# A first weight quarter loaded in fp32 and rounded on the chip, a reordered first group, a compact running state and loads tied to progress, in a linear-attention and Mish feed-forward kernel

## The chip, the core and the metric

The kernel runs on one core of a Trainium2 chip. The metric is the device time of one execution in microseconds (us); the time before is 209.66 us, the median of three runs (209.61 to 210.24).

The names used below are those of the profile: PE is TensorE (matmuls; PEld its weight loads), DVE is VectorE, ACT is ScalarE, POOL is GpSimd, SP is SyncE. ACT, SP and POOL also issue DMAs, each in its own queue; only the loads issued by POOL change the type on the way (fp32 in memory, fp16 on the chip).

## The reference

Per batch b (4) and head h (8), with 768 positions of 64 values, lightning attention in blocks with a decay lam[h]:

```
intra = (q_block @ k_block.T) * Dmask            # Dmask[i,j] = lam^(i-j) for i >= j, else 0
out   = intra @ v_block + (q_block * lam^(i+1)) @ state
state = lam^block * state + (k_block * lam^(block-1-i)).T @ v_block
```

The heads are then laid side by side (x: 3072 tokens x 512) and go through

```
h = x @ w_in          # 512 -> 2048
g = h * tanh(softplus(h))          # Mish
out = g @ w_out       # 2048 -> 512, fp32
```

## The kernel before

**Groups.** The sequence is cut into six groups n = 0..5 of 128 positions (C); a group has one chunk for each of the four batches, chunk number i = 4n + b, so a group is 512 tokens (GT). For each group the loop at line 719 runs 16 units of the first product (`mm1_unit`, ni = 0..15: four matmuls of 512 columns, then ACT's Mish into `hsg`) and then the second product: 16 `mm2_unit` in group 0, and in the later groups 14 `fast_unit`, a scheme with seven instead of eight products whose sums of tokens (`gsum`, line 572) and of weights (`tsum`, line 553) are made by DVE. Everything is in an order written out by hand (`manual_schedule`): each engine executes its instructions in the order in which the program names them. While group n's units run, the attention of group n+1 is made in pieces, put behind the units that the table `room` names; unit u of the loop is an mm1 unit for u < 16.

**First group (lines 682 to 713).** Chunk 0's k and q come in fp32 by SP's and ACT's queues and are rounded by ACT (k0) and DVE (q0). For each chunk c there are three steps: `first_t(c)` transposes k and q on PE, with copies by ACT (pkT) and DVE (pqT); `first_s(c)` makes the scores and DVE multiplies them by the decay mask dm (two sb); `first_o(c)` multiplies by v, and ACT copies the result to x^T (xt). `busy(m)` is m matmuls of 512 columns on zeros. After the steps, the first three chunks' part of units 0 and 1 (`mm1_part`) is done before the loop begins. The tables dm, lk (decay of k), lbc and lbm (decay of the state over a group) are made in between.

**Weights and loads.** w_in's first quarter comes in three parts (win0, line 93), then three more quarters of w_in (line 96) and four of w_out (line 103), all by POOL's queue behind the loads of chunks 0 to 3; then chunks 4 to 7. Group 2's loads (`ahead`) are issued one behind each `att_a` and the rest (v) after group 0's units; those of group n+2 (`later`) behind the units in `times`.

**Running state.** For each batch and half of the heads, `wst[b][hf]` holds two copies of 128 x 256: two pairs of heads, each a block-diagonal 128 x 128, whose blocks off the diagonal are zero. The new state is (pv + old) * lbm: DVE adds (line 302 in group 1, line 393 later: `raw`, 128 x 256), POOL multiplies by lbm (line 304, held back in the list `behind`; line 395 later). In the groups from 2 on, attention goes by pairs of batches: `pair_a` (pv and the state; for n > 2 also `turn` of the chunk two further), `pair_s` (scores; state times q), `pair_o` (times v, scaling to xtok, and a transposing DMA by SP into xt). `turn(i)` is `scale_k(i)`, k times lk, by DVE or POOL according to i (line 264), and two transposing DMAs by SP of q and k.

**PSUM.** The tags ph and po have two buffers each. Unit 2 of every group takes its buffer from po (line 491); the pv of `pair_a` come from po as well while u < 15.

## Time and profile before

| what | us |
|---|---|
| time, median of three runs | 209.66 |
| the profiled execution's own time | 210.5 |
| its span in the profile | 208.5 |
| group 0's first steps, up to the last v product (line 249) | 0 to 19.6 |
| group 0's mm1 units | to 33.9 |
| group 0's mm2 units, with group 1's attention | to about 56 |
| group 1's mm1 units, with group 2's attention | to 75.85 |
| group 1's fast units | to 88.5 |
| groups 2 and 3, each mm1 and fast units | 88.5 to 119.3 and 119.3 to 150.1 |
| groups 4 and 5 | to 208.5 |

Times inside the profile are microseconds from the start of the span. A row of the timeline gives start, duration, engine, line, operation, names and shapes, how many, and in brackets how long the engine stood idle before it and what ended that. A row of the stretches gives, for each engine in the order PE, PEld, DVE, ACT, POOL, the time it was busy and the instructions (x), then the granted TensorE clock as a share of full speed, the mean busy share of the DMA engines and GB/s. A row of the chain gives start, duration and what the chain stood on.

### The profile page before, as it was taken

How to read it: one execution, taken by the hardware profiler on the slowest of the kernel's cores; microseconds unless marked ns; L12 is line 12 of the kernel's file. 1: busy time of each engine (PE TensorE's matmuls, PEld its weight loads, DVE VectorE, ACT ScalarE, POOL GpSimd, SP SyncE). 2: the span in 40 equal slices, each digit the busy share in tenths (PEclk: the TensorE clock that was granted, in tenths of full speed). 3: DMA queues.
4: the chain of work that ended last, by engine and by line, in shares of the span. 5: the costliest groups of instructions: out<-in, count | busy, mean ns of one | idle time of the engine just before them, and what ended most of it. 6: DMA issues, size and time to landing. Idle time of an engine off the chain costs nothing.

```text
span 208.5 us, 4364 instructions
## 1 busy us (share of the span) xinstructions
PE 197.3 (95%) x1736; PEld 128.6 (62%) x1736; DVE 136.5 (65%) x253; ACT 90.2 (43%) x159; POOL 108.5 (52%) x132
## 2 busy tenths in 40 slices
PE   7598999999998999999999999999999999999993
PEld 2366544467644568845578845578755598544892
DVE  5747761577899998546997537995728784222543
ACT  4444768566672532044542055442065520366300
POOL 7997333799999799539997049970000000000000
PEclk9759999999999999999999999999999999999999
DMA  9999999999999399997999994999462222400023
GB/s 128 137 153 176 208 206 195 153 211 131 160 183 165 25 95 137 196 204 157 100 129 148 210 174 69 98 141 199 104 176 53 50 41 75 139 0 3 2 78 124
DMA packets 112470, 26.76 MB, mean 128 GB/s; under 512 B 102594, under 2 KB 111938, under 8 KB 112450
## 3 DMA queue, kind: packets, MB, share of 16 engines
q0 software_dynamic: 78080, 13.37, 87.7%
q1 hardware_dynamic: 31392, 10.49, 26.4%
q10 hardware_dynamic: 2978, 2.62, 4.1%
q8 instruction: 13, 0.21, 0.4%
q14 instruction: 7, 0.06, 0.1%
HBM read 27.26 MB, written 6.29 MB: 161 GB/s over the span
## 4 chain that ended last, share of the span: by engine, by line
PE 73%; DVE 12%; DMA 6%; issue 4%; POOL 2%; ACT 1%; ACTq 0%; DVEq 0%
PE ph L494 28%; PE z L599 13%; PE x L599 8%; PE y L599 7%; PE po L516 6%; DMA vz<-in_v_dram 4%; DVE sb L427 3%; DVE raw L393 2%; DVE xtok L446 2%; DMA qn<-in_q_dram 2%; PE fin L599 2%; DVE gsum L572 1%; PE pO L249 1%; PE pO L438 1%; PE pS L411 1%
## 5 line engine op out<-in xcount | busy, mean ns | idle before, releaser
L494 PE MATMUL ph<-xt,win 128*128 128x512 f16 (+2 forms) x404 | 88.6, 369 | 0.4 <-ACT hsg L508 0.2
L508 ACT ACTIVATE hsg<-ph 128x512 f16<-128x512 f32 x96 | 57.0, 597 | 70.4 <-PE ph L494 70.3
L494 PEld LDWEIGHTS <-win 128*128 128x128 f16 x404 | 37.0, 98 | 37.6 <-issue 0.6
L599 PEld LDWEIGHTS <-gsum 128*128 128x128 f16 x336 | 31.6, 98 | 3.5
L395 POOL TENSOR_TENSOR w<-raw,lbm 128x256 f16<-128x256 f32 x24 | 18.6, 805 | 16.7 <-DVE raw L393 16.7
L427 DVE TENSOR_TENSOR sb<-pS,maskT 128x512 f16<-128x512 f32 x32 | 19.8, 680 | 9.8 <-PE pS L411 9.8
L572 DVE TENSOR_TENSOR gsum<-hsg 128x1024 f16<-128x1024 f16 x20 | 18.6, 932 | 10.9 <-ACT hsg L508 10.9
L599 PEld LDWEIGHTS <-hsg 128*128 128x128 f16 x240 | 23.2, 98 | 3.7
L80 POOL DMA_DIRECT2D vz<-in_v_dram x24 | 21.9, 916 | 4.5 <-DMA win<-in_moe_w_in_dram 2.5
L69 POOL DMA_DIRECT2D kn<-in_k_dram x23 | 21.0, 914 | 4.9 <-DMA win<-in_moe_w_in_dram 2.4
L77 POOL DMA_DIRECT2D qn<-in_q_dram x23 | 20.9, 908 | 4.5 <-DMA wout<-in_moe_w_out_dram 3.3
L599 PE MATMUL x<-wout,hsg 128*128 128x256 f16 x160 | 19.6, 273 | 0.0
L599 PE MATMUL z<-tsum,gsum 128*128 128x256 f16 x160 | 19.1, 272 | 0.0
L264 DVE TENSOR_TENSOR ktil<-kn,lk 128x512 f16<-128x512 f16 (+1 forms) x12 | 11.3, 960 | 6.5 <-DMA kn<-in_k_dram 6.5
L516 PE MATMUL po<-wout,hsg 128*128 128x512 f16 x64 | 15.1, 379 | 0.0
L264 POOL TENSOR_TENSOR ktil<-kn,lk 128x512 f16<-128x512 f16 x12 | 13.2, 1103 | 0.0
L446 DVE TENSOR_TENSOR xtok<-pO,lqt 128x256 f16<-128x256 f32 x32 | 11.3, 412 | 0.9 <-PE pO L438 0.9
L393 DVE TENSOR_TENSOR raw<-pv,w 128x256 f32<-128x256 f32 x24 | 8.6, 414 | 4.6 <-PE pv L385 4.4
L516 PEld LDWEIGHTS <-hsg 128*128 128x128 f16 x64 | 6.0, 98 | 5.9
L599 PE MATMUL z<-tsum,hsg 128*128 128x256 f16 x80 | 9.6, 273 | 0.0
L650 DVE TENSOR_TENSOR u<-z,p 128x512 f32<-128x512 f32 x5 | 3.5, 692 | 9.0 <-PE z L599 9.0
L165 PE MATMUL busy<-kzero 128*128 128x512 f16 x18 | 7.9, 534 | 1.2 <-DVE kzero L150 1.2
(101 smaller groups left out, 220.1 us busy)
## 6 DMA issues: line engine op xcount, KB each, us to landing
out_dram<-osum SPq DMA_DIRECT2D x14, 256.0 KB, 2.5
vz<-in_v_dram POOLq DMA_DIRECT2D x24, 128.0 KB, 5.5
kn<-in_k_dram POOLq DMA_DIRECT2D x23, 128.0 KB, 5.4
qn<-in_q_dram POOLq DMA_DIRECT2D x23, 128.0 KB, 5.5
wout<-in_moe_w_out_dram POOLq DMA_DIRECT2D x4, 512.0 KB, 17.2
win<-in_moe_w_in_dram POOLq DMA_DIRECT2D x3, 512.0 KB, 10.9
out_dram<-osum ACTq DMA_DIRECT2D x5, 256.0 KB, 4.5
out_dram<-osb ACTq DMA_DIRECT2D x4, 256.0 KB, 5.9
```

The source lines that it names most:

```text
L69: nc.gpsimd.dma_start(out=kn[i], in_=chunk_rows(k, i))
L77: nc.gpsimd.dma_start(out=qn[i], in_=chunk_rows(q, i))
L80: nc.gpsimd.dma_start(out=vz[i % NVB][:, :, 0:D], in_=chunk_rows(v, i))
L264: (nc.vector if i <= B or 2 * B < i < 3 * B or i >= (NG - 1) * B else nc.gpsimd).tensor_tensor(out=t, in0=kn[i], in1=bc(lk, 2, D), op=ALU. ...
L395: nc.gpsimd.tensor_tensor(out=wst[b][hf][(n + 1) % 2], in0=raw, in1=lbm[:, hs, :], op=ALU.mult)
L427: nc.vector.tensor_tensor(out=s.sb[m][t], in0=sc[m][t], in1=bc(maskT, 1, JP), op=ALU.mult)
L446: nc.vector.tensor_tensor(out=xtok[m][:, :, t, :], in0=s.pO[t][:, m], in1=bc(lt[:, :, t], 2, D), op=ALU.mult)
L494: nc.tensor.matmul(ph_t[ni][:, lo:hi], win0[min(ni, 2)][:, kc, max(ni - 2, 0) * 128 : max(ni - 2, 0) * 128 + 128] if ni < w else win[ni // ...
L508: nc.scalar.activation(hsg[n][:, ni, :], ph_t.pop(ni), AF.Mish)
L516: nc.tensor.matmul(po, hsg[n][:, ki, b * C : (b + 1) * C], wout[part][:, kk, :], start=(ki == 0), stop=(ki == NKI - 1),)
L572: nc.vector.tensor_tensor(out=gsum[n, i][:, ks, :], in0=a, in1=b, op=op)
L599: nc.tensor.matmul(t, lhs(kk, b), rhs(kk, c, c + w), start=(fresh and kk == 0 and (alone or i == 0)), stop=(kk == HK - 1), skip_group_chec ...
```

## The change

1. **w_in's first quarter.** The three DMAs of POOL are gone. SP issues four DMAs of 128 x 512 fp32 (256 KB each, one for each kc) into `stage` right behind k of chunk 0. DVE rounds kc = 0 and 1 and ACT kc = 2 and 3 into `win[0]`, in the midst of the first steps. The tile `stage` takes one of the two buffers of hsg.
2. **First group.** lk and a new table lbh (lam^128 for every head) are made by ACT before k0; lbc is copied from lbh by DVE, and `pair_decays` goes behind the steps. Seven of the eight decays of the mask stand ahead of q0's rounding, one behind it. The load of the Mish table goes from behind chunk 1's pkT ahead of it. `busy` of 128 columns is added around chunk 0's transposes; of the seven `busy` groups of 512 columns (12 matmuls) two (3 matmuls) stay. Instead, units 0 and 1 are done by chunks of 128 tokens as soon as each chunk's xt is there, and unit 2's first three chunks go behind the last v product.
3. **Compact state.** In groups from 1 on only the blocks on the diagonal are added (`sum_rows`: two DVE instructions of 64 partitions, one for each head of a pair), into a tile `raw` for two batches, and one DVE instruction of 128 x 512 (`next_state`) multiplies it by lbc and writes `state`. POOL's multiplications and `behind` are gone.
4. **scale_k** goes to POOL for i = 5..8 only; i = 12..19, with POOL before, go to DVE.
5. **Loads.** ek's iota goes ahead of q of chunk 1. In groups 1 to 3 each load in `later` has `pace()` ahead of it: POOL copies one element of the latest marked result (an hsg, p1, p7 or u3), and so waits for it. Order within a group: k and q of three chunks first, v later.
6. **Unit 2's buffer** is from po only in groups 0 and 1, else from ph. In group 1 the pieces stand behind the units 6, 8, 11, 12, 16, 20 instead of 6, 8, 9, 12, 13, 17.

The diff, cut to its core:

```diff
-    win0 = [const.tile([128, NKC, b_ - a_], F16, name=f"win0{a_}") for a_, b_ in zip(cuts, cuts[1:])]
+    win = [const.tile([128, NKC, DF // WS], F16, name=f"win{s}") for s in range(WS)]
...
     load_q(0)
+    stage = work.tile([128, 2 * NKC, DF // WS], F32, name="stage", tag="hsg", bufs=2)
+    for kc in range(NKC):
+        nc.sync.dma_start(out=stage[:, kc, :], in_=moe_w_in[kc * 128 : (kc + 1) * 128, 0 : DF // WS])
...
-    for s in range(WS):
+    for s in range(1, WS):
         load_win(s)
...
-        (nc.vector if i <= B or 2 * B < i < 3 * B or i >= (NG - 1) * B else nc.gpsimd).tensor_tensor(
+        (nc.gpsimd if B < i <= 2 * B else nc.vector).tensor_tensor(
...
+    def sum_rows(n, b, pv, j0, nj, olds):
+        if (n, b // 2) not in raws:
+            raws[n, b // 2] = work.tile([128, 2, JP, D], F32, name="raw", tag="raw", bufs=2)
+        raw = raws[n, b // 2]
+        for hp in range(2):
+            rs = slice(64 * hp, 64 * hp + 64)
+            nc.vector.tensor_tensor(out=raw[rs, b % 2, j0 : j0 + nj, :], in0=pv[rs, :, rs],
+                                    in1=olds(rs), op=ALU.add)
+    def next_state(n, p):
+        nc.vector.tensor_tensor(
+            out=state[p][(n + 1) % 2], in0=raws[n, p],
+            in1=lbc.unsqueeze(1).unsqueeze(3).broadcast_to([128, 2, JP, D]), op=ALU.mult)
...
+    def pace():
+        nc.gpsimd.tensor_copy(paced, mark[-1])
...
-            ph_t[ni] = ps.tile([128, GT], F32, name="ph", tag="po" if ni == 2 else "ph", bufs=2)
+            ph_t[ni] = ps.tile([128, GT], F32, name="ph", tag="po" if ni == 2 and n < 2 else "ph", bufs=2)
...
     nc.scalar.activation(k0, kn[0], AF.Copy)
-    decays(0)
+    decays(0, range(JP))
+    decays(1, range(JP - 1))
     nc.vector.tensor_copy(q0, qn[0])
+    decays(1, range(JP - 1, JP))
...
-    first_t(0)
+    busy(2, C)
+    first_t(0, between=4)
     nc.scalar.activation(dm[:, 1], dm[:, 1], AF.Exp)
+    nc.scalar.preload_act_table(AF.Mish)
     busy(1)
+    nc.vector.tensor_copy(win[0][:, 0, :], stage[:, 0, :])
     first_s(0)
-    pair_decays()
-    nc.scalar.activation(lk, lnb, AF.Exp, scale=ek)
-    busy(2)
     first_t(1)
-    nc.scalar.preload_act_table(AF.Mish)
-    busy(1)
+    busy(2)
+    nc.vector.tensor_copy(win[0][:, 1, :], stage[:, 1, :])
+    for kc in (2, 3):
+        nc.scalar.activation(win[0][:, kc, :], stage[:, kc, :], AF.Copy)
     first_s(1)
     first_o(0)
-    busy(3)
     first_t(2)
-    busy(1)
+    for ni in range(2):
+        mm1_part(0, ni, 0, C)
     first_s(2)
     first_o(1)
-    busy(3)
     first_t(3)
+    for ni in range(2):
+        mm1_part(0, ni, C, 2 * C)
+    first_s(3)
     first_o(2)
-    busy(1)
-    first_s(3)
-    mm1_part(0, 0, 0, GT - C)
+    for ni in range(2):
+        mm1_part(0, ni, 2 * C, 3 * C)
     first_o(3)
-    mm1_part(0, 1, 0, GT - C)
+    mm1_part(0, 2, 0, GT - C)
     scale_k(0)
+    pair_decays()
...
-            room = dict.fromkeys((6, 8, 9, 12, 13, 17) if n == 1 else (2, 5, 7, 9, 12, 16), 1)
+            room = dict.fromkeys((6, 8, 11, 12, 16, 20) if n == 1 else (2, 5, 7, 9, 12, 16), 1)
...
             if later and u in times:
+                pace()
                 later.pop(0)()
...
+            if n == 1 and u < 2:
+                next_state(n, u)
             if n == 1 and u < 3:
                 turn((n + 1) * B + 1 + u)
-            while n == 1 and behind:
-                behind.pop(0)()
```

88 lines of the change are left out of this document (40 added, 48 removed).

## Prediction

> **What bounds the kernel now.** I read the page first (busy shares, the chain of work by engine), then the chain in order of time, then the stretches.
>
> ```profile
> PE 197.3 (95%) x1736; PEld 128.6 (62%) x1736; DVE 136.5 (65%) x253; ACT 90.2 (43%) x159; POOL 108.5 (52%) x132
> PE 73%; DVE 12%; DMA 6%; issue 4%; POOL 2%; ACT 1%; ACTq 0%; DVEq 0%
> ```
>
> PE is the bound over the whole, but a busy PE is not a PE at its peak, and 27% of the chain lies elsewhere. So the question is where PE waits. In the chain in order of time:
>
> ```profile
> 1.31 4.05 DMA qn<-in_q_dram
> 5.81 1.05 DVE dm L184 x4
> 9.10 0.18 DVE lnp L192
> 9.41 0.29 ACT lk L694
> 11.81 1.28 PE busy L165 x3
> 15.57 0.65 PE busy L165 x3
> 19.04 0.55 PE pO L249 x7
> 28.68 5.18 PE ph L494 x24
> ```
>
> The first 19.59 us (19.04 + 0.55) are a chain of small steps: a load, decays, small tables, dummy matmuls. From there on PE streams: 24 matmuls of 512 columns in 5.18 us, 0.216 us each, so 0.054 us for 128 columns. The stretches show where it streams less well:
>
> ```profile
> 4.60:8.00 3.40, 1.76 (x19) 1.03 (x20) 2.08 (x7) 1.92 (x4) 3.40 (x5) 1.00 2.32 148
> 8.00:14.85 6.85, 6.02 (x46) 3.86 (x44) 3.39 (x8) 3.36 (x6) 6.85 (x10) 0.50 2.06 142
> 19.60:33.86 14.26, 14.22 (x85) 7.20 (x84) 9.10 (x24) 9.44 (x16) 5.03 (x6) 1.00 1.24 207
> 57.00:75.85 18.85, 16.86 (x164) 8.96 (x163) 18.85 (x29) 9.12 (x16) 17.45 (x21) 1.00 1.18 116
> 88.50:106.40 17.90, 17.30 (x162) 9.05 (x161) 13.05 (x23) 8.87 (x15) 14.26 (x18) 1.00 1.31 152
> 119.30:137.20 17.90, 17.31 (x162) 9.00 (x160) 13.16 (x24) 8.96 (x15) 14.36 (x18) 1.00 1.21 122
> 150.10:166.00 15.90, 15.90 (x145) 7.95 (x143) 9.71 (x18) 8.96 (x15) 0.00 (x0) 1.00 0.44 101
> ```
>
> The last three are the same part (16 units with attention beside) of groups 2, 3 and 4. Group 4 needs no pv, which is 16 matmuls of 128 columns, 0.9 us. So 17.90 - 15.90 - 0.9 = 1.1 us of waiting in each of groups 2 and 3, where the busy column admits 0.60: a tail of each matmul covers part of a gap. In group 1 (57.00 to 75.85) PE is idle 18.85 - 16.86 = 1.99 us by the row; in the same ratio (1.1 to 0.60) that is 3.6 us, and DVE is busy all the time. What PE waits for there:
>
> ```profile
> 62.78 0.38 PE L385 MATMUL pv<-vz,ktil 128*128 128x128 f16 x4 [0.42 <-DMA vz<-in_v_dram]
> 66.02 0.40 PE L411 MATMUL pS<-qraw,kraw 64*128 64x128 f16 x7 [0.40 <-DVE raw L393]
> 91.99 0.38 PE L385 MATMUL pv<-vz,ktil 128*128 128x128 f16 x4 [0.46 <-ACT hsg L508]
> 103.61 0.29 PEld L419 LDWEIGHTS <-qraw 64*128 64x128 f16 x15 [0.24 <-DVE xtok L446]
> 99.27 2.96 DVE L572 TENSOR_TENSOR gsum<-hsg 128x1024 f16<-128x1024 f16 x1
> 99.55 3.26 POOL L395 TENSOR_TENSOR w<-raw,lbm 128x256 f16<-128x256 f32 x4
> ```
>
> The fourth row waits for a scaling that stands behind the fifth: a sum of tokens that takes 2.96 us while POOL's state products (sixth) run. After 150.1 there is almost nothing to win.
>
> **The change, part by part.**
>
> *The first group (term A).* Its root is q of chunk 0. Removed from the chain: lnp and lk with their waits (9.02 to 9.70 in the chain), three of the four decays behind q0 (0.79 us), and most dummy matmuls. But the new limit is what the steps read: the loads of chunks 1 to 3.
>
> ```profile
> 8.14 0.89 POOL L77 DMA_DIRECT2D qn<-in_q_dram  x1
> 9.01 1.78 POOL L80 DMA_DIRECT2D vz<-in_v_dram  x2
> DMA to landing us min/median/max: 4.0/4.8/17.5
> 10.74 2.28 POOL L93 DMA_DIRECT2D win<-in_moe_w_in_dram  x3
> win<-in_moe_w_in_dram POOLq DMA_DIRECT2D x1, 256.0 KB, 6.4
> kn<-in_k_dram POOLq DMA_DIRECT2D x23, 128.0 KB, 5.4
> 15.04 1.29 DVE L239 TENSOR_TENSOR sb<-pS,dm 128x512 f16<-128x512 f32 x2 [0.64 <-PE pS L235]
> ```
>
> The third row is that of q's loads in the first 40 us. So q of chunk 3 is there at 8.14 + 4.0 = 12.1 us, while PE first asks for it behind the dummies that end at 16.2 (15.57 + 0.65): a cover of 4 us, which goes. The four stage DMAs now run ahead of these loads on the same engines. Their price has no row. In the stretch 19.60 to 33.86 w_in and w_out flow at 207 GB/s of fp16, 0.52 MB in 2.5 us, for 1 MB read. In fp32 the read is the same and the write double: 2.5 us if the read limits, 5.0 if the write does, nothing if gaps take it in; I take 2.5, as that row is the same matrix in pieces of the same 2 KB. Then q of chunk 3 comes at 14.6. Behind it: its four transposes (0.22) and their way to DVE (0.17: the row 19.04 has 0.55 for seven matmuls), the copy (0.43), scores (as much as transposes, 0.39), two sb (1.29), units 0 and 1's third part, eight matmuls of 128 columns that now stand ahead on PE (0.4), and the v product (0.55): 18.1 us against 19.59, so 1.5 us. Besides, 24 matmuls of 128 columns of units 0 and 1 are then done (1.3 us) where before four of 384 (0.65) were: 0.7 us. Unit 2's part hides ACT's last xt as unit 1's did. A = 2.2 us. The rounding costs DVE and ACT two instructions each:
>
> ```profile
> 5.38 0.43 DVE L686 CAST q<-qn 128x512 f16<-128x512 f32 x1 [0.82 <-DMA qn<-in_q_dram]
> 4.18 0.63 ACT L684 ACTIVATE k<-kn 128x512 f16<-128x512 f32 x1 [0.79 <-DMA kn<-in_k_dram]
> 5.20 1.09 POOL L77 DMA_DIRECT2D qn<-in_q_dram  x1
> ```
>
> 0.86 on DVE and 1.26 on ACT lie in the wait for chunk 1 and 2's loads, if the stage has landed; behind them on DVE wait the sb, on ACT pkT and xt. That cover is gone if the loads are early; then they are on the chain, with at most 0.86. Bounds of A: 4 us if stage costs the loads nothing and the clock stays full, -0.3 if it costs 5.0.
>
> The third row is POOL's issue during the cast of q0: 1.09 us, where others take 0.89. The Trainium skill, page SBUF — State Buffer, section "SBUF: two separate sides", says that a VectorE copy from fp32 in SBUF can lock GpSimd out of writing descriptors. By it the two casts would put 0.4 us on the loads, and A would be 1.8; the sum does without.
>
> *Later weights.* Three DMAs less in POOL's queue: v of chunk 3, the last ahead of them, lands at about 13.9 (issued 9.9, half of the row 9.01 on, plus 4.0), win0's last part, issued at 12.2, at 18.6: 4.7 us of transfer go and 2.5 come, so all from w_in's second quarter on is 2.2 us earlier, like PE. The tightest is k of chunk 4:
>
> ```profile
> 38.51 0.69 DVE L264 TENSOR_TENSOR ktil<-kn,lk 128x512 f16<-128x512 f16 x1 [6.50 <-DMA kn<-in_k_dram]
> 41.25 0.31 PEld L324 LDWEIGHTS <-ktil 128*128 128x128 f16 x2
> ```
>
> It is ready at 39.20 for a use at 41.25: 2 us of cover. Without the 2.2, A would be lost here by 0.2 only.
>
> *Group 1 and the state (term B).* The costs, POOL's first:
>
> ```profile
> L395 POOL TENSOR_TENSOR w<-raw,lbm 128x256 f16<-128x256 f32 x24 | 18.6, 805 | 16.7 <-DVE raw L393 16.7
> L393 DVE TENSOR_TENSOR raw<-pv,w 128x256 f32<-128x256 f32 x24 | 8.6, 414 | 4.6 <-PE pv L385 4.4
> L572 DVE TENSOR_TENSOR gsum<-hsg x20: 675/682/2960, 69.3 to 193.3; 128x1024 f16<-128x1024 f16 x20
> L264 DVE TENSOR_TENSOR ktil<-kn,lk x12: 681/685/2184, 18.9 to 151.4; 128x512 f16<-128x512 f16 x11, 128x512 f16<-128x512 f32 x1
> ```
>
> For each group POOL loses eight products (6.4 us). DVE has as many sums as before (four of 256 columns for two batches) and two next_state of 128 x 512, which I price as the median ktil, 0.69: 1.4 us. In group 1's own halves two sums of 128 columns (0.26 each, as L184 in the chain) stand for one of 256 (0.41): 0.1 in each of eight halves, 0.9 in all, nothing unless DVE is what comes last there. What comes back: DVE's instructions beside POOL's products take up to three to four times their median (maxima 2960 and 2184). In 57.00 to 75.85 three ktil, four sums of weights and two of tokens are stretched, by some 4 us, against 1.4 added. Of PE's 3.6 us, about 1 is order on PE itself (as in group 4, where short gaps remain), 0.6 is the load of v; of the other 2, which wait for DVE or for a buffer that DVE holds (the new places 11, 16, 20 ease that too), I take B = 1.5; bounds 0 and 3. v's load is 2.2 us earlier as PE is, and POOL issues it without products between.
>
> *Groups 2 and 3 (term C).* Unit 2 in ph frees both po buffers for pv: the wait for hsg (0.46 idle) goes. The sum of tokens in 0.68 instead of 2.96 lets xtok be ready before PE asks, also with next_state ahead of it. DVE gets 2 x 0.69 (next_state) and 2 x 0.69 (scale_k) in 17.90 us, 2.8, and loses 2.3: 13.6 of 17.90 busy, so hidden. Of 1.1 us each I take 0.8: C = 1.6; bounds -1 (DVE's additions reach PE) and 2.2.
>
> *Pacing and scale_k.* A copy of one element and a wait on POOL; behind it wait only loads. POOL's products are gone, so loads are issued at PE's pace. The tightest is k of chunk 15: issued behind u3 of group 1 (row below), at 84.3 to 85.2, landing after the 5.4 of kn's row at about 90, scaled behind the first two sums of group 3's pair_a, at about 92.5 (the pv row 91.99).
>
> ```profile
> 83.58 0.69 DVE L650 TENSOR_TENSOR u<-z,p 128x512 f32<-128x512 f32 x1 [1.12 <-PE z L599]
> ```
>
>  The pacing costs nothing; without that cover, as much as k is late. The marks end with step 3, so the last four loads of a group aren't paced.
>
> *Sum.* A + B + C = 2.2 + 1.5 + 1.6 = 5.3 us. The profiled execution's own 210.5 (span 208.5, 2.0 around it) becomes 205.2; the median is 0.84 below it, so 209.66 - 5.3 = **204.4 us**.
>
> **The rivals.**
>
> 1. *The loads hold the first group* (0.15): stage's transfer costs 5.0 us. A = -0.3, so 206.9. For it: the fp32 write is double. Against: in the row of 207 GB/s the read is already twice that.
> 2. *The clock stays full* (0.14): the row 8.00 to 14.85 has a granted clock of 0.50, after a stretch in which PE was busy 1.76 of 3.40 us. Full clock there, with loads hardly delayed, gives A = 4: 202.6. For it: more matmuls stand in 4.6 to 8. Against: fewer stand after 9. The Trainium skill, page TensorE: Matmul & The Clock Gate, section "Part 1: The HAM clock gate", says that a window of about 3.4 us of sustained work frees the clock and an idle one halves it; the rows agree with such windows (3.40 and 6.85), and by it this rival hangs on the one window from 4.6 us.
> 3. *DVE becomes the bound in the middle* (0.11): stretching is due to POOL's issues too and stays. C = 0, B = 0.5: 207.0. For it: DVE is at 18.85 of 18.85 in group 1. Against: the median of gsum is 0.68 while POOL issues loads most of the time.
> 4. *Slower: a scale_k on DVE waits for a paced load* (0.07). Place: k of chunks 14, 15, 18, 19 in pair_a. Behind it on DVE stand the sums that free PE's pv buffers. It decides from a landing 8 us after the issue; each us beyond is lost in groups 2 and 3. With 4 us: A + B = 3.7 won, C lost, 8 lost: 214.0. For it: landings up to 17.5 us in the qn row. Against: that was behind the weights; the median of kn is 5.4.
>
> **How the numbers follow.** Forecast 0.53, rivals 0.15, 0.14, 0.11, 0.07. The forecast's own range is 202.8 to 206.0. For 8 in 10 I go to rivals 1, 2 and 3, with their bounds: 201.2 to 207.7. All but rival 4 are faster by more than 0.3% (about what a measurement here can tell from no change); with some of 1 and 3 that fall short: faster 0.89, same 0.04, slower 0.07.
>
> **What would show it.** A: the last v product ends near 18 us, q of chunk 3 lands near 14.6, and PE's first wait in the steps is for DMA. B: stretch of group 1's units 2 us shorter, no ktil or gsum over 1 us. C: 16.8 us where 17.90 stand, no wait of pv for hsg. Wrong if: v product after 19.6; DVE waiting for kn; the 17.90 unchanged.

## The result and the profile after

The changed kernel is slower: 211.96 us (median of 9 runs, 210.69 to 213.18) against 210.24 for the kernel before (9 runs, 208.26 to 211.84), a ratio of 1.0122 with a 95% interval of 1.0086 to 1.0158. (The ratio, here and below, compares the executions in the fast state alone, so it is not the quotient of the two medians.) The forecast was 204.4 from 209.66, with a range to 207.7. The profiled execution of the changed kernel took 213.18 us, the longest of its nine; its span is 210.8.

First the page of the changed kernel (busy time and share by engine), which stands against the first row that the prediction shows:

```profile
PE 197.4 (94%) x1753; PEld 129.9 (62%) x1753; DVE 139.0 (66%) x281; ACT 91.2 (43%) x161; POOL 81.7 (39%) x125
```

POOL lost its products as meant (108.5 to 81.7 us), DVE gained 2.5 us, PE does the same work. So the sum of work tells nothing here; only the stretches do. I cut both traces at the same events: the last matmul of the last v product, the last of group 0's mm1 units, and the first mm1 matmul of each later group. The stretches of the changed kernel (length, busy time of PE, PEld, DVE, ACT, POOL, clock, DMA share, GB/s):

```profile
0.00:20.85 20.85, 15.23 (x136) 10.02 (x137) 13.23 (x34) 10.03 (x17) 15.79 (x26) 1.00 1.54 181
20.85:34.61 13.76, 13.60 (x87) 7.03 (x85) 9.45 (x27) 9.19 (x16) 5.26 (x6) 1.00 1.27 205
34.61:55.83 21.22, 20.82 (x179) 12.70 (x178) 13.98 (x33) 13.17 (x29) 19.11 (x21) 1.00 2.18 161
55.83:88.75 32.92, 31.58 (x320) 21.79 (x317) 28.88 (x55) 13.38 (x25) 13.16 (x24) 1.00 1.25 121
88.75:122.36 33.61, 31.49 (x288) 21.08 (x289) 22.84 (x43) 11.35 (x19) 14.34 (x24) 0.95 1.73 142
122.36:152.01 29.65, 29.65 (x290) 20.36 (x288) 23.23 (x43) 11.35 (x19) 14.05 (x24) 1.00 1.44 137
```

and those of the kernel before for the end of group 0 with group 1's halves, then groups 1, 2 and 3:

```profile
33.48:54.08 20.60, 20.58 (x178) 12.64 (x177) 12.44 (x26) 13.15 (x29) 17.05 (x19) 1.00 2.07 164
54.08:88.55 34.47, 32.29 (x320) 22.16 (x318) 30.61 (x47) 13.38 (x25) 30.76 (x36) 1.00 1.59 138
88.55:119.25 30.70, 30.11 (x291) 20.48 (x289) 22.53 (x37) 11.34 (x19) 21.18 (x24) 1.00 1.53 154
119.25:149.95 30.70, 30.11 (x291) 20.48 (x289) 22.30 (x39) 11.34 (x19) 16.81 (x20) 1.00 1.30 134
```

The loss of 2.3 us of span is a sum of large terms of both signs: +1.5 to the last v product, -0.35 in the rest of group 0's mm1 units, +0.6 in the stretch of group 1's halves (21.22 against 20.60), -1.5 in group 1, **+2.9 in group 2**, -1.05 in group 3. Group 4 lasts 28.76 us in both, and 0.3 are lost in group 5.

**Where the first group waits.** PE's rows of the changed kernel's first steps (start, duration, what, and the idle time before it with what ended it):

```profile
7.34 0.61 PE L213 MATMUL pq<-ident,q 128*128 128x128 f16 x4 [1.65 <-DVE q L704]
10.02 0.61 PE L213 MATMUL pk<-ident,kn 128*128 128x128 f16 x4 [0.95 <-DMA kn<-in_k_dram]
11.44 0.61 PE L213 MATMUL pq<-ident,qn 128*128 128x128 f16 x4 [0.82 <-DMA qn<-in_q_dram]
14.63 0.63 PE L213 MATMUL pq<-ident,qn 128*128 128x128 f16 x4
17.22 0.39 PE L213 MATMUL pq<-ident,qn 128*128 128x128 f16 x4
20.02 0.61 PE L506 MATMUL ph<-xt,win 128*128 128x128 f16 x8 [0.69 <-ACT xt L249]
20.46 0.61 PE L247 MATMUL pO<-sb,vz 128*128 128x128 f16 x8
```

The waits for loads are for q of chunk 0 and for k and q of chunk 1, not for q of chunk 3 (it lands at 16.50, and PE takes it up at 17.22 without a wait). The last wait of all, 0.69 us, is for ACT's copy into xt: chunk 2's part of units 0 and 1 stands ahead of chunk 3's v product on PE. Four transposes take 0.61 to 0.63 us up to 14.63 and 0.39 at 17.22: from these times the clock was halved for the earlier ones (the trace's records of it set in with full clock at 16.4 us). The issues of the first 20 us, with the median from issue to landing as the last number, before and after:

```profile
qn<-in_q_dram POOLq DMA_DIRECT2D x3, 128.0 KB, 4.5
qn<-in_q_dram ACTq DMA_DIRECT2D x1, 256.0 KB, 4.0
```

```profile
stage<-in_moe_w_in_dram SPq DMA_DIRECT2D x4, 256.0 KB, 6.9
qn<-in_q_dram POOLq DMA_DIRECT2D x3, 128.0 KB, 8.7
qn<-in_q_dram ACTq DMA_DIRECT2D x1, 256.0 KB, 5.2
```

**Where group 2 waits.** PE's two waits from 86 to 100 us in the changed kernel, the piece of the chain that ends the second, and SP's queue:

```profile
88.75 2.75 PE L506 MATMUL ph<-xt,win 128*128 128x512 f16 x12 [0.61 <-DMA xt<-xtok]
96.98 0.40 PE L417 MATMUL pS<-qraw,kraw 64*128 64x128 f16 x8 [2.12 <-DMA kraw<-ktil]
```

```profile
89.66 7.28 DMA kraw<-ktil
```

```profile
74.16 10.63 SPq L454 DMA_TRANSPOSE xt<-xtok  x4
84.89 1.23 SPq L271 DMA_TRANSPOSE qraw<-qn  x1
86.22 1.32 SPq L271 DMA_TRANSPOSE kraw<-ktil  x1
88.27 1.29 SPq L271 DMA_TRANSPOSE qraw<-qn  x1
89.66 1.71 SPq L271 DMA_TRANSPOSE kraw<-ktil  x1
```

The transpose of k of chunk 13 went out at 88.05 before, half a us ahead of group 2's first unit (88.55); now it goes out at 89.66, 0.9 us behind it (88.75), and needs 7.28 us to land. Behind this wait the clock halves:

```profile
98.35:101.75 3.40, 3.40 (x16) 1.76 (x14) 2.40 (x6) 1.19 (x2) 0.32 (x2) 0.50 2.06 148
```

Group 2 less group 3 is 33.61 - 29.65 = 3.96 us: 2.1 of waiting and about 1.7 from 3.4 us at half clock. Not every execution has this half clock: in six of the nine the granted clock over the span is 0.997 or more, where one such stretch would leave 0.992. The median of these six is 211.7 us, so the loss does not hang on it.

### The profile page after: what moved, and what is told of

Its sections match the earlier page's. It is cut to its first block, busy times and chain, and to the rows that moved or that the text cites. A ratio compares the mean times of both kernels' runs of the same rounds, so it can differ in the third digit from the quotient of the medians.

```text
span 210.8 us, 4428 instructions
## 1 busy us (share of the span) xinstructions
PE 197.4 (94%) x1753; PEld 129.9 (62%) x1753; DVE 139.0 (66%) x281; ACT 91.2 (43%) x161; POOL 81.7 (39%) x125
## 4 chain that ended last, share of the span: by engine, by line
PE 76%; DVE 9%; DMA 8%; ACT 2%; issue 1%; SPq 1%; POOL 1%; ACTq 0%; POOLq 0%
PE ph L506 34%; PE z L611 12%; PE x L611 7%; PE y L611 6%; PE po L528 6%; DMA qn<-in_q_dram 4%; DMA kraw<-ktil 3%; DVE sb L433 2%; DVE raw L285 2%; DVE gsum L584 2%; PE fin L611 2%; PE pO L444 2%; PE pS L417 2%; PE pO L247 1%; PE pv L395 1%
## 5 line engine op out<-in xcount | busy, mean ns | idle before, releaser
L506 PE MATMUL ph<-xt,win 128*128 128x512 f16 (+2 forms) x424 | 90.6, 364 | 1.9 <-ACT xt L249 0.9
L506 PEld LDWEIGHTS <-win 128*128 128x128 f16 x424 | 38.9, 99 | 40.1 <-issue 4.1
L80 POOL DMA_DIRECT2D vz<-in_v_dram x24 | 21.1, 884 | 6.2 <-DMA win<-in_moe_w_in_dram 2.0
L69 POOL DMA_DIRECT2D kn<-in_k_dram x23 | 20.6, 897 | 6.3 <-issue 1.9
L77 POOL DMA_DIRECT2D qn<-in_q_dram x23 | 20.3, 884 | 7.0 <-DMA wout<-in_moe_w_out_dram 3.3
L584 DVE TENSOR_TENSOR gsum<-hsg 128x1024 f16<-128x1024 f16 x20 | 13.6, 686 | 10.9 <-ACT hsg L519 10.9
L496 POOL COPY paced<-hsg 1x1 f16<-1x1 f16 x23 | 6.6, 288 | 31.2 <-ACT hsg L519 31.2
L262 DVE TENSOR_TENSOR ktil<-kn,lk 128x512 f16<-128x512 f16 (+1 forms) x20 | 13.6, 686 | 3.9 <-DMA kn<-in_k_dram 3.7
L285 DVE TENSOR_TENSOR raw<-pv,state 64x256 f32<-64x256 f32 x24 | 10.1, 421 | 7.8 <-PE pv L395 7.4
L648 DVE TENSOR_TENSOR osum<-y,u 128x512 f32<-128x512 f32 x8 | 5.5, 689 | 4.4 <-PE y L611 4.4
L584 DVE TENSOR_TENSOR gsum<-hsg,gsum 128x1024 f16<-128x1024 f16 x10 | 6.5, 688 | 2.7 <-PE z L611 2.7
```

Source lines behind the costliest of these rows:

```text
L69: nc.gpsimd.dma_start(out=kn[i], in_=chunk_rows(k, i))
L77: nc.gpsimd.dma_start(out=qn[i], in_=chunk_rows(q, i))
L80: nc.gpsimd.dma_start(out=vz[i % NVB][:, :, 0:D], in_=chunk_rows(v, i))
L262: (nc.gpsimd if B < i <= 2 * B else nc.vector).tensor_tensor(out=t, in0=kn[i], in1=bc(lk, 2, D), op=ALU.mult)
L285: nc.vector.tensor_tensor(out=raw[rs, b % 2, j0 : j0 + nj, :], in0=pv[rs, :, rs], in1=olds(rs), op=ALU.add)
L506: nc.tensor.matmul(ph_t[ni][:, lo:hi], win[ni // w][:, kc, (ni % w) * 128 : (ni % w) * 128 + 128], xt[n][:, kc, lo:hi], start=(kc == 0), s ...
```

## Experiments

My theories after the comparison: the fp32 transfer holds the first group back (**load**) against the new order itself (**order**); group 2's wait comes from where SP issues the transposes (**late issue**), from the unit table (**room**), from the bunched loads (**pace**) or from DMA engines with too much to do (**full engines**); the halves' 0.6 us come from the **split sums**.

All runs in one table, the stretches from one profiled execution each, in us (a profiled execution can lie 2 us off the median of its run: 210.96 against 208.94 in e11, 210.05 against 208.18 in e6); "v" is the start of the last v product's last matmul, "to end" is from there to the end of the span, the ratio is to the kernel before, from the runs' times.

| run | v | halves | group 1 | group 2 | group 3 | to end | ratio, 95% interval |
|---|---|---|---|---|---|---|---|
| before | 19.37 | 20.60 | 34.47 | 30.70 | 30.70 | 189.1 | 1 |
| changed | 20.85 | 21.22 | 32.92 | 33.61 | 29.65 | 190.0 | 1.0122 (1.0086 to 1.0158) |
| e1_old_room | 21.51 | 21.22 | 33.77 | 33.84 | 29.65 | 191.5 | 1.0275 (1.0234 to 1.0317) |
| e2_no_pace | 20.26 | 21.21 | 34.15 | 32.10 | 29.65 | 189.9 | 1.0160 (1.0108 to 1.0212) |
| e3_old_start | 19.96 | 21.22 | 32.57 | 33.00 | 30.17 | 189.8 | 1.0020 (0.9985 to 1.0054) |
| e4_new_start | 20.18 | 20.60 | 33.15 | 32.67 | 30.71 | 190.0 | 1.0121 (1.0087 to 1.0155) |
| e5_early_turn | 20.97 | 21.21 | 33.93 | 29.66 | 29.81 | 187.5 | 1.0062 (1.0027 to 1.0097) |
| e6_less_load | 21.18 | 21.22 | 32.15 | 30.80 | 29.75 | 187.1 | 0.9927 (0.9894 to 0.9959) |
| e7_full_sum | 20.07 | 20.60 | 32.80 | 33.64 | 29.75 | 189.6 | 1.0020 (0.9986 to 1.0055) |
| e8_stage_dma | 22.38 | 20.60 | 34.29 | 30.72 | 30.70 | 189.0 | 1.0137 (1.0091 to 1.0184) |
| e9_order | 16.84 | 20.71 | 36.29 | 31.22 | 30.71 | 191.7 | 1.0015 (0.9978 to 1.0052) |
| e10_old_start_turn | 18.17 | 20.61 | 36.77 | 29.65 | 30.30 | 190.3 | 1.0006 (0.9965 to 1.0047) |
| e11_old_start_turn21 | 20.21 | 20.61 | 35.70 | 29.91 | 30.38 | 189.0 | 0.9967 (0.9923 to 1.0012) |
| e12_order_turn | 17.28 | 20.61 | 38.56 | 29.65 | 30.56 | 192.3 | 1.0000 (0.9956 to 1.0045) |
| e13_order_early_v | 16.29 | 21.04 | 35.17 | 31.22 | 30.70 | 191.8 | 0.9990 (0.9966 to 1.0014) |
| e14_order_early_v_turn21 | 16.29 | 21.03 | 34.95 | 29.72 | 30.73 | 190.1 | 0.9881 (0.9842 to 0.9920) |
| e15_order_early_v_split | 16.64 | 21.21 | 33.31 | 30.90 | 30.15 | 189.1 | 0.9858 (0.9827 to 0.9889) |
| e16_unit2_buffer | 18.08 | 20.60 | 34.41 | 29.92 | 29.66 | 187.0 | 0.9878 (0.9835 to 0.9922) |

### The start: transfer or order

**e8_stage_dma**, the transfer alone, in the kernel before (it is added and not used: the quarter still comes by POOL's queue as well):

```diff
     load_q(0)
+    stage = work.tile([128, 2 * NKC, DF // WS], F32, name="stage", tag="hsg", bufs=2)
+    for kc in range(NKC):
+        nc.sync.dma_start(out=stage[:, kc, :], in_=moe_w_in[kc * 128 : (kc + 1) * 128, 0 : DF // WS])
```

> The kernel before with the four fp32 DMAs of w_in's first quarter added by SP's queue and not used (work added, nothing left out). Theory load: q of chunk 1 lands at about 11 us in place of 9.9, v of chunk 3 at 17.5 to 18 in place of 13.9, the last v product ends 1 to 1.5 us later, and the time is 1 to 1.5 us over that of the kernel before. Rival order (the changed order of the steps, not the transfer, costs the time): the last v product stays within 0.4 us of 19.4 and the time within 0.5 us.

Measured: 1.37% slower, the last v product 3.0 us later, everything behind it as before (189.0 us to the end against 189.1). PE's rows:

```profile
7.57 0.40 PE L220 MATMUL pq<-ident,q 128*128 128x128 f16 x4 [2.61 <-DVE q L689]
11.95 0.61 PE L220 MATMUL pq<-ident,qn 128*128 128x128 f16 x4 [0.99 <-DMA qn<-in_q_dram]
22.05 0.55 PE L252 MATMUL pO<-sb,vz 128*128 128x128 f16 x7 [0.37 <-DVE sb L242]
```

The transfer by itself costs twice what I expected of this run: PE has q of chunk 1 at 11.95 us (8.44 before), and the steps that follow run at half clock until 18.15 us (14.84 before).

**e9_order**, the other half: the new order, but w_in's first quarter by POOL's queue as before, and units 0 and 1 done where they were (by chunks they need the stage, so that part is tested only together with it).

```diff
-    decays(0)
+    decays(0, range(JP))
+    decays(1, range(JP - 1))
     nc.vector.tensor_copy(q0, qn[0])
...
     first_t(3)
-    first_o(2)
     busy(1)
     first_s(3)
+    first_o(2)
     mm1_part(0, 0, 0, GT - C)
     first_o(3)
```

> The kernel before with the changed order of the first steps, but without the fp32 transfer: w_in's first quarter comes by POOL's queue in three parts as before, and the units are done where they were (one matmul group on zeros stands where the units by chunks stood). Theory load (the order gains what the prediction said, and the transfer takes it and more): the last v product ends at 18.0 to 18.5 us in place of 19.4 and the time is about 1 us under that of the kernel before. Rival order: the v product ends at 19.4 or later and the time is no lower; then the new order is itself without gain.

Measured: the v product comes 2.5 us earlier than before (16.84), more than either theory had; but the time is the same, 1.0015 (0.9978 to 1.0052). PE's rows of the steps, and then of group 1:

```profile
7.20 0.40 PE L217 MATMUL pk<-ident,kn 128*128 128x128 f16 x4
16.45 0.61 PE L251 MATMUL pO<-sb,vz 128*128 128x128 f16 x8
61.06 0.38 PE L387 MATMUL pv<-vz,ktil 128*128 128x128 f16 x4 [0.94 <-DMA vz<-in_v_dram]
62.48 0.38 PE L387 MATMUL pv<-vz,ktil 128*128 128x128 f16 x4 [1.04 <-DMA vz<-in_v_dram]
67.48 0.38 PE L387 MATMUL pv<-vz,ktil 128*128 128x128 f16 x4 [1.13 <-DVE sb L429]
```

Transposes of chunk 1 start at 7.20, without a wait, at full clock (0.40 us for four). So the order is right and the transfer is what spoils it. One trace each would not show this, since v varies by 2.1 us with the same start (18.08 to 20.21 in the five runs with the old one); but the five runs with the new order and without the transfer have 16.29 to 17.28, and the seven with both 20.07 to 21.51. The medians are 19.37, 16.64 and 20.85: 2.7 us won by the order, 4.2 lost by the transfer and what hangs on it (the rounding, the units by chunks). And e9's gain is given back 40 us later: group 1 waits for v of chunks 8 and 9 and then for DVE, and lasts 36.29 us in place of 34.47. POOL issues v of chunk 8 at 52.42 us (53.49 before), but it lands at 61.01 (60.94 before).

**e4_new_start** (the whole new start on the kernel before) and **e3_old_start** (the old start under all the rest) are the same split in the other direction; their edits are the diff's parts 1 and 2, put in and taken out.

> The kernel before with the changed first group alone: fp32 transfer of w_in's first quarter, the new order of the first steps, units 0 and 1 by chunks; state, loads later on and table as before. Theory load: the last v product ends at about 21, the first product of group 0 at about 35.0, and the kernel is 1.1 us slower than before, all of it in the first 35 us. Rival by the prediction: the start gains 2 us and what loses lies elsewhere: the kernel is 1 to 2 us faster than before.

> The changed kernel with the first group, its loads and w_in's first quarter as before; compact state, pacing, units and table as changed. The last v product ended at 19.59 before and at 21.07 in the changed kernel, the end of group 0's first product 33.86 and 34.99. Theory load (the fp32 transfer of the first quarter shares the DMA engines with the first chunks and holds them back by 4 us): here these are 19.6 and 33.9 again, and the time is about 1.1 to 1.5 us under the changed kernel's. Rival, that the new start costs nothing at the end because a later wait takes it up: the time stays within 0.4 us.

Measured: e4 has 1.0121, the whole loss of the change, from the start alone; e3 has 1.0020, 1.0% (2.1 us) under the changed kernel. Theory load holds in sign, but "all of it in the first 35 us" was wrong: in e4 the end of group 0's first product is at 33.94, 0.5 us late, and group 2, with the old code, lasts 2.0 us longer than before (32.67): it, too, waits for a transpose of k (0.73 us) and for xt (1.13). Why a start that is later by half a us ends in such waits is not shown: in e8, 3.0 us later, there are none.

### The halves: split sums

**e7_full_sum**:

```diff
-            sum_rows(n, b, s.pv, 2 * hf, 2, lambda rs: w[rs, :, rs])
+            raw = work.tile([128, 2, 128], F32, name="rawf", tag="rawf", bufs=7)
+            nc.vector.tensor_tensor(out=raw, in0=s.pv, in1=w, op=ALU.add)
+            behind.append(lambda: scaled(b, hf, raw))
...
+        for hp in range(2):
+            rs = slice(64 * hp, 64 * hp + 64)
+            nc.gpsimd.tensor_tensor(
+                out=state[b // 2][0][rs, b % 2, 2 * hf : 2 * hf + 2, :], in0=raw[rs, :, rs],
+                in1=bc(lbc[rs, 2 * hf : 2 * hf + 2], 2, D), op=ALU.mult)
```

> The changed kernel, where group 1's eight halves add the whole 128 x 256 with one DVE instruction, as before, and POOL then writes the compact state from the blocks on the diagonal. From the end of group 0's first product to group 1's first full unit it took 20.60 us before and with the changed start alone, and 21.22 in the changed kernel and with the old start under the other changes. Theory split sums (two DVE instructions of 64 partitions take 0.42 us each where one of 128 took about as much, and PE waits for DVE in the halves): 20.6 us again, and the time falls by 0.6 us unless group 2's wait takes it back. Rival, that the 0.62 us come from elsewhere (the loads or the units): it stays at 21.2.

Measured: 20.60 again. (The time falls by 1.0% against the changed kernel, more than these 0.6 us: in the profiled execution the first group is 0.8 us shorter as well.) DVE's sums between 36 and 57 us (count, busy, mean ns), changed kernel and e7:

```profile
L285 DVE TENSOR_TENSOR raw<-pv,w 64x128 f32<-64x128 f32 x16 | 4.5, 283 | 0.1
```

```profile
L316 DVE TENSOR_TENSOR rawf<-pv,w 128x256 f32<-128x256 f32 x8 | 3.3, 415 | 0.0
```

A quarter of the elements (half of the columns on half of the partitions) costs 283 ns against 415. Each half of the heads pays 2 x 283 - 415 = 151 ns more, 1.2 us in eight, and 0.6 reach PE. In all runs the stretch is 20.6 to 20.7 with whole sums (21.0 in e13 and e14, whose loads go out earlier) and 21.2 with split ones: this is shown.

### Group 2: issue, table, pacing or engines

**e1_old_room**, the unit table put back: `(6, 8, 9, 12, 13, 17)` for `(6, 8, 11, 12, 16, 20)`.

> The changed kernel with one table put back: the pieces of group 2's attention stand behind the units 6, 8, 9, 12, 13, 17 of group 1 again. Group 2 lasts 33.77 us in the changed kernel (122.52 less 88.75) and 30.86 before; group 3, with the same units, lasts 29.66. Theory room: the last transposing DMA into xt now is issued at unit 20, the transposes of q and k of chunks 12 and 13 stand behind it in SP's queue, and the scores of group 3 wait 2.12 us for k of chunk 13 while the clock drops to half. By it, group 2 lasts 30 us here, the wait of 0.61 us for xt at its start goes, and the time is 3 to 4 us under the changed kernel's, about 208.3. Rival pace: the loads that were held back and now go out together between 84 and 94 us slow the transposes down. By it, the wait stays within 1 us of its 2.12 and the time changes by less than 1 us.

Both theories miss: the time rises by 1.5% over the changed kernel, and the wait stays. PE's rows:

```profile
75.58 0.73 PE L425 MATMUL pO<-state,qraw 64*128 64x64 f16 x16 [1.04 <-DVE xtok L452]
99.19 0.42 PE L417 MATMUL pS<-qraw,kraw 64*128 64x128 f16 x8 [2.40 <-DMA kraw<-ktil]
```

With the pieces closer together, group 1 waits for DVE, 0.85 us longer in all; against group 2's start the last transpose goes out only 0.35 us earlier (91.24 with a start at 90.68). So the table is not the whole cause of the late issue. With the old table SP is free at 85.29, but the transpose of k of chunk 12 waits until 87.75 for its scaling, which DVE makes at 87.04, behind two sums of the second product (u); before, POOL had made it by 79.99. By these traces either of the two moves, of `pair_o` or of scale_k, keeps the transposes late; no run takes back both. The new table is right for the new kernel.

**e2_no_pace**, without the `pace()` line.

> The changed kernel without the copies by which POOL waits for a result ahead of each later load; the new order of the loads stays. Theory room: group 2's wait for k of chunk 13 stays (over 1.5 us), group 2 lasts over 33 us, the time is within 0.7 us of the changed kernel's. Rival pace: the loads are spread out again, the transposes land earlier, group 2 lasts 31 us or less, the time falls by 2.5 us or more. If both have a part, the wait shrinks to about half.

Groups 1 and 2 together last 66.25 us against 66.53; the waits are spread over xt and two transposes, and the time is not lower (1.0160, its interval overlaps the changed kernel's). Pacing moves the waits about; these runs show neither a cost nor a gain.

**e5_early_turn**:

```diff
-            if n > 0 and n + 2 < NG and u in (23, 25):
-                turn((n + 2) * B + (u - 23) // 2)
+            if n > 0 and n + 2 < NG and u in ((15, 18) if n == 1 else (23, 25)):
+                turn((n + 2) * B + (u > 15 if n == 1 else u > 23))
```

> The changed kernel, with the transposes of q and k of chunks 12 and 13 issued behind the units 15 and 18 of group 1 in place of 23 and 25. In the changed kernel they stand in SP's queue behind the last transposing DMA into xt, and the last of them goes out 0.9 us after group 2 has begun; the scores of group 3 wait 2.3 us for it and the clock then halves for 3.4 us. Theory late issue: with them out of the way earlier, this wait goes, group 2 lasts about 29.7 us (as group 3 does) in place of 33.6, and the time falls by 3 us or more. Rival full engines (the DMA engines are busy from 75 to 94 us, so what goes earlier pushes something else back): the wait moves to the xt of group 2 or to chunks 14 and 15, groups 1 and 2 together still last 65.2 to 66.6 us, and the time changes by less than 1 us.

**e6_less_load**, without the twelve loads of group 3 (`load_k`, `load_q`, `load_v` return at once for 12 <= i < 16).

> The changed kernel without the twelve loads of group 3, issued in group 1: group 3 takes k and q of group 2 and the v that lies in its buffers. Theory full engines: without this traffic the transposes land within 5 us of their issue in place of 7, the wait for k of chunk 13 goes, group 2 lasts about 29.7 us and the time falls by 3 to 4 us. Rival late issue: the transposes go out as late as before and the wait of 2.3 us shrinks by no more than a half.

Measured in e5: SP's queue, the wait that remains, and group 2's stretch:

```profile
78.50 1.96 SPq L271 DMA_TRANSPOSE kraw<-ktil  x1
82.04 1.22 SPq L271 DMA_TRANSPOSE kraw<-ktil  x1
83.35 3.15 SPq L454 DMA_TRANSPOSE xt<-xtok  x2
```

```profile
90.15 2.76 PE L506 MATMUL ph<-xt,win 128*128 128x512 f16 x12 [1.01 <-DMA xt<-xtok]
```

```profile
90.15:119.81 29.66, 29.66 (x289) 20.37 (x289) 22.55 (x42) 11.35 (x19) 14.14 (x24) 1.00 1.57 140
```

Group 2 lasts 29.66 us, as group 3 does, with PE busy in all of it; 1.0 us of the gain of 3.95 goes to group 1, whose end now waits 1.01 us for xt, issued behind these transposes (0.61 in the changed kernel), and which waits 0.72 for DVE's scores at 80.27. So in the trace late issue holds for three quarters, full engines for one. The times do not reach the 3 us that I expected: e5's ratio is 0.6% (1.3 us) under the changed kernel's, and the intervals overlap; the trace's gain has the 1.7 us of the half clock in it, which most executions of the changed kernel don't lose. In e6, which is 2.0% (4.1 us) under the changed kernel with less to load, the transposes go out as late as there (89.79, group 2 starts at 88.71), yet the wait for k of chunk 13 is gone (one of 0.97 us for chunk 14 or 15 remains). The landing times of kraw's transposes between 80 and 106 us, changed kernel and e6:

```profile
DMA to landing us min/median/max: 6.0/7.1/7.3
```

```profile
DMA to landing us min/median/max: 2.4/4.2/6.8
```

Without the loads k of chunks 12 and 13 land 2.45 and 4.20 us after the issue in place of 6.03 and 7.28 (e6's 6.8 is chunk 15, when loads run again). For the wait of 2.1 us both count, late issue *and* shared engines; either remedy takes it away. The issue alone does not set its size: e4 sends this transpose as early as the kernel before, 0.54 us ahead of group 2, and waits 0.73, because it lands after 7.97 us; e3 sends it 1.37 us behind the start and waits only 0.92. The Trainium skill, page DMA: Bandwidth & Descriptors, section "Issuing engines are not separate DMA queues", says that transfers started by different engines run on the same DMA engines and interleave. The trace agrees: POOL's loads slow SP's transposes (7.28 us against 4.20 for k of chunk 13), and SP's stage slows POOL's loads (8.7 against 4.5).

### One line alone

**e16_unit2_buffer**, the kernel before with unit 2's buffer changed, nothing else:

```diff
-            ph_t[ni] = ps.tile([128, GT], F32, name="ph", tag="po" if ni == 2 else "ph", bufs=2)
+            ph_t[ni] = ps.tile([128, GT], F32, name="ph", tag="po" if ni == 2 and n < 2 else "ph", bufs=2)
```

> The kernel before with unit 2's buffer of the groups from 2 on taken from ph in place of po, nothing else changed. Theory buffer: the wait of 0.63 us for pv goes in groups 2 and 3, and these last 30.1 us each in place of 30.70 (0.6 less each), so the time falls by about 1.2 us at most. Rival state: the wait of 0.63 stays or another takes its place, both groups stay at 30.7, and the 1.05 us come from the compact state.

Measured: 0.9878 (0.9835 to 0.9922). The wait of the kernel before in group 3,

```profile
122.69 0.38 PE L385 MATMUL pv<-vz,ktil 128*128 128x128 f16 x4 [0.46 <-ACT hsg L508]
```

is gone in both groups, and the stretches of groups 2 and 3 in e16 are

```profile
87.20:117.12 29.92, 29.92 (x290) 20.37 (x288) 21.92 (x37) 11.34 (x19) 21.28 (x24) 1.00 1.60 156
117.12:146.78 29.66, 29.66 (x291) 20.35 (x289) 21.04 (x39) 11.34 (x19) 16.86 (x20) 1.00 1.27 140
```

0.78 and 1.04 us less, 1.8 together. This buffer, without the compact state, gives group 3's whole gain: POOL still makes its products here, and the wait behind xtok (0.24 in the prediction's row at 103.61) goes with the buffer. The measured 1.2% (2.6 us) is more than the 1.2 us at most that I expected; 1.8 lies within its interval (1.6 to 3.5 us), and whether a rest is real (the clock of the first group, below, could make one) is open.

### The parts together

**e10_old_start_turn** joins e3, e7 and e5; **e11_old_start_turn21** puts chunk 13's transposes behind unit 21 instead of 18; **e12_order_turn** takes e9's start in place of the old one.

> The changed kernel with the start as before, whole sums with POOL's compact state in group 1, and the transposes of chunks 12 and 13 behind the units 15 and 18. If the parts add up as the stretches of the single runs say (to group 0's end 33.5, halves 20.6, group 1 33.9, group 2 29.7, group 3 29.8, then 28.8 and 30.0) the span is 206.3 and the time about 2 us under that of the kernel before. If the full engines set the time of groups 1 and 2, these two last over 65 us and the time is within 0.6 us of before.

> As the run before in this list, but the transposes of chunk 13 stand behind unit 21, so behind the last transposing DMA into xt in SP's queue. Theory order in the queue: the wait for xt at the start of group 2 (1.17 us with both ahead) goes, the wait for k of chunk 13 comes back by less than 1 us since it goes out about 1.5 us earlier than in the changed kernel: groups 1 and 2 together 62.5 to 63.3 us, a time 0.3 to 1 us under the run before. Rival full engines: what xt gains the k of chunk 13 loses, the two groups together as in the run before within 0.3 us.

> The new order of the first steps without the fp32 transfer, whole sums with POOL's compact state in group 1, the transposes of chunks 12 and 13 behind the units 15 and 18, the rest as changed. If the order gains 1 us by itself, the time is about 1 us under that of the run with the old start and the same transposes, and 3 us under the kernel before; if it gains nothing, the two agree within 0.4 us.

e10 and e12 miss: 1.0006 and 1.0000. Group 2 is 29.65 in both, but group 1 lasts 36.8 and 38.6 us: it waits for v of chunks 8 and 9, whose loads now stand behind POOL's products, then for xt (2.45 and 2.04 us). e12's group 1 also has a stretch at half clock, from 63.06 to 66.47, about 1.7 us of its 38.6. e11 is 0.4% under e10, as expected, though the intervals overlap: its wait for xt is 0.60 us, and none for k of chunk 13 is left. But v of chunk 9 alone costs 1.9 us, and groups 1 and 2 together last 65.6 us (66.4 in e10) where I expected 62.5 to 63.3.

**e13_order_early_v** tells whether these loads are the cause; the edit goes with it into e14 and e15:

```diff
         att_w(s)
-        ahead.pop(0)()
+        for _ in range(1 if b < 2 else 2):
+            ahead.pop(0)()
```

> The kernel before with the new order of the first steps, without the fp32 transfer, and with group 2's loads issued two behind each half from chunk 6 on, so that the four v go out with the last halves instead of behind group 0's last unit. Theory v landing: the waits of 0.9 and 1.0 us for v at 60 us and after it go, group 1 lasts 34.3 us or less in place of 36.3, and the time is 1.5 us or more under that of the kernel before. Rival DVE: group 1 stays over 35.5 us, the time stays within 0.7 us of before.

> The new order without the fp32 transfer, group 2's v loads early, whole sums with POOL's compact state in group 1, the transposes of chunk 12 behind unit 15 and of chunk 13 behind unit 21, the rest as in the changed kernel. If the parts add up (group 0's first product ends at 31.5, halves 20.6, group 1 33.0, group 2 29.8, group 3 29.7, then 28.8 and 29.6) the span is 203.0 and the time about 5 us under that of the kernel before. If the DMA engines set the end of group 2 whatever is issued when, the time is within 1.5 us of before.

> As the run before in this list, but with the split sums of the changed kernel in group 1's halves (DVE alone, POOL free). Theory split sums: the halves last 21.2 us, 0.6 us more; group 1 may win back up to that, since POOL's loads are not behind its multiplications. By it the time is 0 to 0.6 us over that of the run before.

In e13 the waits for v are gone, but group 1 only falls from 36.29 to 35.17, and where it waited for v it now waits for DVE:

```profile
61.62 0.38 PE L388 MATMUL pv<-vz,ktil 128*128 128x128 f16 x4 [0.71 <-DVE tsum L556]
```

```profile
56.32 4.16 DVE L266 TENSOR_TENSOR ktil<-kn,lk 128x512 f16<-128x512 f16 x1
```

So v took 1.1 us of the gain; DVE, where one scale_k of 0.69 takes 4.16 us while POOL makes its products, stands right behind it, and the time is that of the kernel before. My expectation of 1.5 us falls, that of the rival (over 35.5 us) nearly holds. **e15 takes 0.9858 (0.9827 to 0.9889), 206.97 us against 209.74**, with group 1 at 33.31. It beats both kernels, and so do e14 and e16. But the three intervals overlap: beside e16's one line, which e14 and e15 contain, all the rest adds nothing that these runs can tell from zero. e14 was to win 5 us and wins 2.5, and e15, which was to be up to 0.6 us slower than e14, is not slower. e15 waits once more for a transpose in group 2:

```profile
101.14 0.40 PE L422 MATMUL pS<-qraw,kraw 64*128 64x128 f16 x8 [1.08 <-DMA kraw<-ktil]
```

In e14's trace the whole sums lose more than the 0.2 us that the halves are shorter: seven buffers for eight sums make DVE wait 2.47 us for POOL at 55.75, and so PE 1.86 us at 56.23.

## Why the prediction was wrong

- **Term A failed, in two steps.** "Then q of chunk 3 comes at 14.6" priced the transfer at 2.5 us and made chunk 3 the limit. The loads landed 4.2 us later (8.7 against 4.5), and q of chunk 3 at 16.50 (the 4.0 in its sum was the least of the row, 4.5 is what this load took before). What PE waited for was chunk 0's and chunk 1's q: the four stage DMAs share the engines with the very first loads, not only with the later ones. So the v product came 1.5 us later where I had it 1.5 earlier, and the first product ended 1.1 us later where I had 2.2 earlier. Rival 1 had the mechanism and, with 5.0, a price near the 4.2, but let it cost only so much that A was -0.3; e8 shows 3.0 us at the v product. The order itself gives 2.5 us (e9), or 2.7 by the medians, where I had 2.2 with the transfer. And the sum for units 0 and 1 has PE's work, 0.4 us, but not the 0.69 that they wait for ACT's xt.
- **The clock** was made a rival for the gain alone. In the seven runs with the fp32 transfer and the new order it is full for good only from 14.7 to 17.5 us on; with the order alone from 4.7 to 9.3 us on (e9, e13, e14, e15; e12 has another half stretch from 15.3 to 18.7). So the late loads seem to cost twice: PE waits, and then runs its steps at half speed. No run separates the two, and the old start, with its loads on time, has the full clock only from 14.8 to 16.0 us on in three of five traces.
- **That a gain is kept** ("From there on PE streams") failed: e9, e10 and e12 start group 1 up to 2 us earlier and end it at most 0.2 us earlier. "v's load is 2.2 us earlier as PE is" was the false step for them: v of chunk 8 landed at 61.01 in e9 and at 62.21 in e10, where POOL issues it behind its products, against 60.94 before.
- **Term B**: group 1 lost 1.54 us, I had 1.5. But e4, with the old code, loses 1.3 there too, so this figure doesn't show the mechanism. e15 against e13 (33.31 against 35.17) is in line with it, but these differ in the table, the pacing and the transposes too: left open. The ktil and gsum rows came out as I said, with the POOL products gone: no more maxima of 2 or 3 us, and a mean equal to the median:

```profile
L584 DVE TENSOR_TENSOR gsum<-hsg 128x1024 f16<-128x1024 f16 x20 | 13.6, 686 | 10.9 <-ACT hsg L519 10.9
L262 DVE TENSOR_TENSOR ktil<-kn,lk 128x512 f16<-128x512 f16 (+1 forms) x20 | 13.6, 686 | 3.9 <-DMA kn<-in_k_dram 3.7
```

  The split sums, "0.9 in all, nothing unless DVE is what comes last there", cost 0.6: DVE is what comes last there.
- **Term C**: group 3 won 1.05 where I had 0.8, by the buffer (e16); the sum of tokens and the compact state add nothing there. Group 2 lost 2.9 where I had a gain of 0.8. The step that failed is that the moves cost nothing in group 2 if DVE's additions are hidden. The change moves `pair_o` to unit 20, and so xt's two last DMAs (81.71 and 82.99 us in place of 79.34 and 80.84), and behind them in SP's queue chunk 13's transposes; and it moves chunk 12's and 13's scale_k behind other sums on DVE (e1). I looked at POOL's and DVE's queues and not at SP's; no rival was made of it.
- **Pacing at nothing**: not contradicted (e2's interval overlaps the changed kernel's). Rivals 3 and 4 didn't happen: gsum stayed at 0.69, and DVE's scale_k waited less for loads than before (3.7 us in all by the row above, 6.5 before).

## What to carry to other kernels

When a transfer is moved to an idle queue, ask whose packets it goes among: the queue was idle, the DMA engines were not, and the first loads of the kernel paid for it. Follow a gain to the next thing that comes at a fixed time (a load, a transpose in a queue); it is won only if that comes earlier as well. And try a bundle's smallest line by itself: here one buffer's tag by itself gave, within the intervals, as much as the best joint version.

## What the runs showed of the hardware

- The **clock of the first group** differs from one execution to the next. With the same old start it went to full for good at 14.84 (before), 15.47 (e3), 15.97 (e11), 9.87 (e10) and 9.60 us (e16), and the v product came at 19.37, 19.96, 20.21, 18.17 and 18.08: 2.1 us of spread that goes with the clock, nearly as much as the whole result. The Trainium skill, page TensorE: Matmul & The Clock Gate, section "Part 1: The HAM clock gate", says that the window of about 3.4 us runs freely and doesn't start with the kernel. The trace agrees: the stretches at half clock are 3.41, 6.83 and 10.24 us long (in group 2 of the changed kernel, in the kernel before, in e8).
- **What a wait costs depends on where it falls.** Behind the first group the clock halved four times, each time for 3.41 us, about 1.7 us lost. The records of the clock lie on a grid of 3.41 us, and PE's busy time in the grid's window ahead of the halving was 1.36 us (changed), 1.01 (e1), 1.27 (e7) and 1.30 (e12): none of the four windows was idle throughout, as the prediction's second rival has it ("an idle one halves it"). With 1.51 (e11), 1.55 (e10) and 1.58 us (e2) it did not halve. e10's wait of 2.45 us and e3's of 2.08 fell across two windows and left the clock full; e12's two waits of 0.65 and 1.61 us fell almost whole into one, and it halved. In the first group, with its short matmuls, 1.77 (before) and 1.93 (e12) were followed by half clock too, so the limit is not one of busy time alone.
- Two transposing DMAs of 128 x 512 fp16 (k of chunks 12 and 13) land 2.45 and 4.20 us after their issue when group 3's loads are away and 6.03 and 7.28 beside them; POOL's loads of 128 KB take 4.5 and 8.7 us beside the fp32 stage.
